# Attention and a gated MLP on one core: batch 2's local attention weights transposed by VectorE and DMA in place of TensorE, with new planner constants

## Chip, core and metric

One core of one Trainium2 chip. The metric is the device time of one execution in microseconds (us). The kernel before took 934.95 us, the median of 3 runs (934.14 to 935.41).

## What is computed

Two things in a row. First, for 8 batches and 8 heads (576 tokens, 64 numbers per head), a pooled attention (queries, keys and values averaged over 4 tokens) and a local attention (each token sees the tokens less than 4 places away) are added. Then the 4608 rows of 512 numbers go through a matrix to 2048 columns, a rational function of each element, and a matrix back to 512.

```python
out_d = sm_attn(q_d, k_d, v_d)                      # pooled by 4
out_up = np.repeat(out_d, factor, axis=2)
mask = np.abs(pos[:, None] - pos[None, :]) < factor
attn = softmax(np.where(mask, scores, -1e9))        # local
out = out_up + attn @ v

h = x @ w_in                                        # 4608x512 @ 512x2048
P = a[0] + a[1]*h + a[2]*h**2 + a[3]*h**3
Q = 1 + |b[0]|*|h| + |b[1]|*h**2
y = (P / (Q + 1e-6)) @ w_out
```

## The kernel before

**The MLP.** The tokens are cut into nine blocks of 512: the first 512 tokens of each of the 8 batches, and one block of all the remainders. A block has 16 steps (144 steps in all), one for each 128 of the 2048 columns. Step n has three parts. `h_part` (L1355 for block 0, with plain f32 operands; L1369 for the others, with each operand split into a high and a low part and three products) makes 128x512 values of h on TensorE (PE). `middle` takes them through six activations on ScalarE (ACT, all of them at L1383: three or four that read PSUM, a logarithm, an exponential) and seven operations on VectorE (DVE, L1399 to L1417); it leaves the high part `g` at L1408 and the low part at L1417. `o_part` (L1435, 12 matmuls) multiplies both into four PSUM banks. The step's `o_part` runs about two steps behind its `h_part`, so that the middle of a step has that long to finish. After a block's 16 steps ACT copies the four banks out (L1479) and SyncE (SP) stores them (L1482).

**The attention.** Batch b's attention is worked in two halves of two head pairs each (class `Half`; pairs a and o), and must end before block b's steps begin, since the block's rows come from it (`split_x`, L1308 on ACT and L1311 on DVE, makes the high and low parts). It is woven into the steps of earlier blocks: batch 2's lies in the steps of block 0's end and of block 1. A half is a chain: scores on PE (L572 or, with the mask added by PE, L562; L856 and L898 where DVE adds the mask), the row maximum on DVE, the exponentials on ACT (L648 from PSUM, L980 from SBUF, five a call, and L674 for the pooled part), the inverse sums (L684, L685) and the normalization on DVE (L730) and ACT (L709). Then the weights must be turned, keys onto the partitions, before PE can multiply them with the values (`weight_both`, one burst).

**Two ways to turn the local weights.** The constant `FLIP` says from which batch on the second way is used; it is 3 before.

- Batches 0 to 2, `turn`: for each pair PE transposes five 128x122 tiles into PSUM (L1033) and ACT copies them to SBUF as `et` (L1081). The weighting matmuls are those of L747.
- Batches 3 to 7, `flip`: the exponentials are written to a tile `eq` in another order of its columns; one DVE instruction transposes it in blocks of 32x32 into `fx` (L1109); SP sends `fx` to DRAM in four transfers (`fd`, L1121) and fetches it back in one (L1126) into `ef`, where each block stands at its place. The weighting matmuls are those of L741.

The pooled weights are transposed by PE in both (L1039 in `turn`, L1138 in `turn_pooled`). In batch 2 the mask is added by PE (`PEMASK`), before and after.

**What sets the order.** All operations are first recorded as tasks of a planner (`Plan`), each with an engine, a duration, the rooms that it reads and writes, and perhaps a due time. `Plan.run` places them on the engines one by one: of those that are ready on an engine, the one with the earliest latest-start time. What comes out is a fixed order of instructions for each engine; the due times are not looked at on the chip. The due time of step n's `h_part` is `due_h(n)`, which advances by `H_STEP` for each step after the 16th; `SPLIT_EARLY` and `ENDS` say how long before a block's first step its rows must stand ready, and `SCORES_EARLY` how long before that the two scores pieces are due. `FLIPSP` and `FLIPLAG` are what the planner takes for SP's issue of the four `fd` transfers and for the landing of `fd` and `ef`:

```python
            there = Room(None, [("D", c.b % 2, c.odd)])
            add("SP", FLIPSP, leave, (x,), (there,), lag=FLIPLAG[0])
            add("SP", 0.7, back, (there,), (y,), lag=FLIPLAG[1])
```

```python
            if b >= FLIP:
                for c in half_.cs:
                    half_.flip(c)
                half_.turn_pooled(bk)
                if q == 0:
                    todo_.append(begin_half(b, 1))
                elif b + 1 < B and AHEAD_S:
                    begun.append(begin_half(b + 1, 0))
            else:
                half_.turn(bk, bk, bk, lent[2])
```

Of the kernel before, what the change touches and what calls it, by code (L numbers as in the profile page):

```python
# [273 lines left out]
def attention_moe(  # L274
# [322 lines left out]
    def softmax_local(c, bk):  # L597
# [43 lines left out]
        def exps(j):  # L641
            for k in range(NW // 2):
                n = 2 * k + c.pos(j)
                dst, src = s.el.ap[:, k, c.pos(j), :], view[:, j, k, :]
                if c.b >= FLIP:
                    n = 5 * c.pos(j) + k
# [55 lines left out]
    def normalize(c):  # L702
# [22 lines left out]
        by = sm[:, :NW].unsqueeze(2).broadcast_to([P, NW, D])  # L725
        if c.b >= FLIP:
            e, by = s.eq.ap, sm[:, :NW].unsqueeze(1).unsqueeze(3).broadcast_to([P, 2, NW, QD])
# [6 lines left out]
    def window(c, x, w, o):  # L734
# [3 lines left out]
        for j in range(2):  # L738
            m = c.pos(j) * D
            if c.b >= FLIP:  # L740
                mms.append(nc.tensor.matmul(  # L741
# [74 lines left out]
    class Half:  # L816
# [22 lines left out]
        def scores(self, c, bk):  # L839

            flip = c.b >= FLIP

# [17 lines left out]

            add("PE", 0.95, issue, (c.slot.qk,), bk, due=self.due - SCORES_EARLY[c.odd] if c.b >= LATER else None)
            if c.b >= FLIP:
                n = NW // 2 * QD
# [20 lines left out]
        def scores_rest(self, bk):  # L884
# [32 lines left out]
            def issue():  # L917
# [17 lines left out]
                "PE", SREST, issue, (o.slot.qk, *(c.slot.pq for c in self.cs)), (*bk, bc),  # L935
                due=self.due - SCORES_EARLY[1]
            ).step = ROOM[0]
# [22 lines left out]
        def softmax(self, c):  # L960
            s = c.slot
            nm, sm = s.nm.ap, s.sm.ap
            if c.b >= FLIP:
                e, axis = s.eq.ap.rearrange("p b n k -> p n b k"), mybir.AxisListType.XY
# [139 lines left out]
        def flip(self, c):  # L1104
# [25 lines left out]
# [4 lines that stand above are left out]
# [154 lines left out]
    def due_h(n):  # L1288
        m = blocks[0].nstep
        return H0 + H_FIRST * min(n, m) + H_STEP * max(0, n - m)  # L1290

# [5 lines left out]
    def split_x(k, due=None):  # L1297
        blk = blocks[k]
        due = due or due_h(blk.first) - SPLIT_EARLY
        t = blk.t  # L1300
# [21 lines left out]
    def ahead(n):  # L1322
        return AHEAD * min(1.0, max(0, n - blocks[-1].first) / RAMP)
# [95 lines left out]
    def o_part(n, f, subs=range(4)):  # L1419
# [3 lines left out]
        fc = s * blk.fg + f  # L1423
        due = due_h(n) + O_LAG * H_STEP + 0.25 * f
        order = [[(m, sub) for m in (0, 2)] for sub in range(blk.nsub)] + [[(1, sub)] for sub in range(blk.nsub)]
        if n >= NS - KEEP:
            order = [[(m, sub) for m in (0, 2, 1)] for sub in subs]
            due = due_h(n) - ahead(n) + O_LAG * H_STEP + 20.0 * subs[0]
        for q, what in enumerate(order):
# [125 lines left out]
    def attend(b):  # L1555

        early, gap = (SPLIT_EARLY, QUAD_GAP) if b < LATER else ENDS
        last = due_h(blocks[b].first) - early - 3.0
# [38 lines left out]
    def begin_half(b, q):  # L1597
        early, gap = (SPLIT_EARLY, QUAD_GAP) if b < LATER else ENDS
        last = due_h(blocks[b].first) - early - 3.0
        bk = banks[0:2]  # L1600
        half_ = Half(b, q, last - (1 - q) * gap)
        half_.load()
        c = half_.cs[0]
        if b in PEMASK:
            scores(c, bk)
            softmax_local(c, bk)
        else:
            half_.scores(c, bk)
        return half_
# [75 lines left out]
O_LAG = 2.09  # L1685
H0 = 20.57
H_FIRST = 6.27
H_STEP = 6.13
SPLIT_EARLY = 8.0
QUAD_GAP = 42.0  # L1690
LATER = 2
ENDS = (8.0, 41.3)
SCORES_EARLY = (47.4, 41.0)
WARM = 0.6
EP_DVE = (1, 3)
LEAD = 13.84
# [16 lines left out]
SREST, ABOTH = 1.7, 2.2  # L1713
ROOM = (1.2, 1.2, 0.6)
LENT = (3, 2, 99)
FLIP = 3
AHEAD_S = 1
FLIPLAG = (2.5, 3.0)
FLIPSP = 2.4


_OUTS = [((NT, DM), "float32")]
# [69 lines left out]
```

## Time and profile before

| what | us |
|---|---|
| median of 3 runs (lowest, highest) | 934.95 (934.14, 935.41) |
| the profiled execution: its time | 936.64 |
| its span, first to last instruction | 934.8 |
| PE busy in the span | 920.8 |
| DVE busy | 852.0 |
| ACT busy | 784.2 |
| GpSimd (POOL) busy | 117.9 |

The span is what the profile's rows add up to; the profiled execution's own time lies 1.84 us above it, and 1.69 us above the median. "Busy" is the time in which an engine worked on at least one instruction. Matmuls follow each other faster than one takes (the next starts while the last drains), so what a row of PE costs is read from the start of one to the start of the next, and the same holds for short instructions on DVE and ACT.

### The profile page before, as it was taken

The page shows a single profiled execution, that of the slowest core. Times are in us where ns is not written, and L with a number is a line of the kernel's source. Part 1 is how long each engine was busy: PE and PEld are TensorE (multiplying, and loading weights), DVE is VectorE, ACT ScalarE, POOL GpSimd, SP SyncE. Part 2 cuts the span into 40 slices and gives each one's busy share as a digit, 9 for nine tenths or more (in the row PEclk, how much of TensorE's full clock was granted, in tenths as well). Part 3 has the DMA queues.
Part 4 walks back from the last instruction along what each step waited for, and adds up shares of the span by engine and source line. Part 5 has one row for each costly group of instructions (what it writes and reads, how often), then busy time and mean ns, then how long its engine had stood idle before and what let it go on. Part 6 is the DMA issues. An engine that isn't in the chain of part 4 may idle for free.

```text
span 934.8 us, 19294 instructions
## 1 busy us (share of the span) xinstructions
PE 920.8 (99%) x7149; PEld 728.7 (78%) x7149; DVE 852.0 (91%) x1381; ACT 784.2 (84%) x1906; POOL 117.9 (13%) x140
## 2 busy tenths in 40 slices
PE   8999999999999999999999999999999999999997
PEld 6666667788878888788878888888788888888886
DVE  8899999999879899889989998999898999988994
ACT  5899997989797979888897979797988887778772
POOL 3122021111120202020111112020201000000000
PEclk9999999999999999999999999999999999999999
DMA  9987453333464545363445436454522210001001
GB/s 319 325 265 186 138 129 73 102 73 90 101 131 119 101 126 125 95 123 96 112 112 143 77 98 136 114 105 120 129 73 45 57 46 1 1 0 46 1 1 45
DMA packets 58973, 97.62 MB, mean 104 GB/s; under 512 B 7744, under 2 KB 39552, under 8 KB 58880
## 3 DMA queue, kind: packets, MB, share of 16 engines
q1 hardware_dynamic: 41008, 76.30, 25.3%
q0 software_dynamic: 17728, 19.96, 15.5%
q8 instruction: 56, 0.92, 0.4%
q14 instruction: 37, 0.30, 0.1%
q10 hardware_dynamic: 144, 0.13, 0.0%
HBM read 80.38 MB, written 15.99 MB: 103 GB/s over the span
## 4 chain that ended last, share of the span: by engine, by line
PE 79%; ACT 13%; DVE 4%; issue 2%; DMA 1%; SPq 0%; DVEq 0%; ACTq 0%
PE psum L1435 36%; PE psum L1369 34%; ACT m L1383 5%; ACT eq L980 2%; ACT gb L1383 2%; PE psum L1355 2%; PE psum L741 1%; ACT epc L674 1%; ACT el L648 1%; PE psum L1189 1%; PE psum L1138 1%; PE psum L856 1%; DMA qk<-in_qk_dram 1%; DVE wb L472 1%; ACT xf L1479 1%
## 5 line engine op out<-in xcount | busy, mean ns | idle before, releaser
L1435 PE MATMUL psum<-wh,g 128*128 128x512 f32 x1072 | 364.9, 403 | 3.5 <-DVE g L1408 2.2
L1369 PE MATMUL psum<-xs,wh 128*128 128x512 f32 x1024 | 260.1, 392 | 0.0
L1383 ACT ACTIVATE m<-psum,cf 128x512 f32<-128x512 f32 x288 | 214.2, 751 | 37.9 <-PE psum L1369 28.2
L1435 PEld LDWEIGHTS psum<-wh,g 128*128 128x128 f32 x1072 | 200.3, 188 | 57.6 <-DVE g L1408 6.5
L1369 PEld LDWEIGHTS psum<-xs,wh 128*128 128x128 f32 x1024 | 191.0, 188 | 41.0 <-DVE xs L1311 0.3
L1435 PE MATMUL psum<-wl,g 128*128 128x512 f32 x536 | 209.7, 391 | 0.1
L1369 PE MATMUL psum<-xs,wl 128*128 128x512 f32 x512 | 138.4, 392 | 0.0
L1383 ACT ACTIVATE gb<-m,cf 128x512 f32<-128x512 f32 x134 | 100.8, 752 | 44.7 <-DVE m L1399 42.4
L1435 PEld LDWEIGHTS psum<-wl,g 128*128 128x128 f32 x536 | 100.8, 188 | 22.6 <-issue 2.3
L1383 ACT ACTIVATE gb<-psum,cf 128x512 f32<-128x512 f32 x134 | 107.9, 806 | 6.3 <-PE psum L1435 6.2
L1408 DVE TENSOR_TENSOR g<-m,m 128x512 fp32r<-128x512 f32 x134 | 92.1, 687 | 21.3 <-ACT m L1383 15.3
L1369 PEld LDWEIGHTS psum<-xs,wl 128*128 128x128 f32 x512 | 95.2, 188 | 20.4 <-issue 0.4
L1399 DVE SCALAR_TENSOR_TENSOR m<-m,cf,m 128x512 f32<-128x512 f32 x144 | 107.4, 746 | 2.9 <-ACT m L1383 2.7
L528 POOL DMA_DIRECT2D pq<-in_qkp_dram x84 | 75.2, 942 | 221.8 <-DMA pq<-in_qkp_dram 135.2
L1416 DVE TENSOR_TENSOR m<-m,m 128x512 f32<-128x512 f32 x144 | 99.2, 689 | 1.8
L1404 DVE TENSOR_TENSOR m<-m,m 128x512 f32<-128x512 f32 x144 | 98.5, 684 | 0.9 <-ACT m L1383 0.7
L1405 DVE TENSOR_TENSOR m<-m,gb 128x512 f32<-128x512 f32 x134 | 92.1, 687 | 3.6 <-ACT gb L1383 0.6
L1417 DVE TENSOR_TENSOR g<-m,m 128x512 fp32r<-128x512 f32 x134 | 91.8, 685 | 3.3 <-PE psum L747 0.5
L1383 ACT ACTIVATE m<-gb 128x512 f32<-128x512 f32 x134 | 87.9, 656 | 7.7 <-DVE m L1404 6.5
L1411 DVE SCALAR_TENSOR_TENSOR m<-m,g 128x512 f32<-128x512 f32 x134 | 92.0, 686 | 2.1
L1383 ACT ACTIVATE m<-psum 128x512 f32<-128x512 f32 x144 | 88.5, 615 | 0.0
L528 POOL DMA_DIRECT2D vpc<-in_vp_dram x42 | 35.5, 846 | 363.7 <-DMA vpc<-in_vp_dram 266.2
(118 smaller groups left out, 1052.0 us busy)
## 6 DMA issues: line engine op xcount, KB each, us to landing
qk<-in_qk_dram SPq DMA_DIRECT2D x32, 590.0 KB, 4.7
pq<-in_qkp_dram POOLq DMA_DIRECT2D x84, 144.0 KB, 3.4
vw<-in_vw_dram SPq DMA_DIRECT2D x32, 320.0 KB, 3.8
out_dram<-xf SPq DMA_DIRECT2D x35, 256.0 KB, 4.0
vpc<-in_vp_dram POOLq DMA_DIRECT2D x42, 168.0 KB, 3.5
fd<-fx SPq DMA_DIRECT2D x80, 80.0 KB, 1.8
ef<-fd SPq DMA_DIRECT2D x20, 320.0 KB, 2.9
sx<-in_w_in_dram SPq DMA_DIRECT2D x5, 1024.0 KB, 11.3
```

Source lines behind the costliest of these rows:

```text
L528: lambda d=dst, x=x: nc.gpsimd.dma_start(out=d.ap, in_=x, accum_op=ALU.add),
L980: nc.scalar.activation(out=e[:, n], in_=e[:, n], func=AF.Exp, bias=nm[:, n : n + 1], scale=scale, accum_out=sm[:, n : n + 1],)
L1369: nc.tensor.matmul(ph.ap[:, f * t : (f + 1) * t], lhsT=(high, low)[j][0][fc].ap[:, c, :], rhs=blk.x[i].ap[:, c, :] if blk.b is not None el ...
L1383: return add("ACT", cost, lambda: nc.scalar.activation(out=to, in_=in_, func=func, **kw), (room_in, cf, *more), (out_,))
L1399: lambda: v.scalar_tensor_tensor(out=tb.ap, in0=tq.ap, scalar=b1, in1=tb.ap, op0=ALU.mult, op1=ALU.add),
L1404: add("DVE", 0.61, lambda: v.tensor_tensor(out=ta.ap, in0=ta.ap, in1=tq.ap, op=ALU.mult), (ta, tq), (ta,))
L1405: add("DVE", 0.61, lambda: v.tensor_tensor(out=ta.ap, in0=ta.ap, in1=u, op=ALU.add), (ta, gh), (ta,))
L1408: add("DVE", 0.61, lambda: v.tensor_tensor(out=gh.ap, in0=ta.ap, in1=tq.ap, op=ALU.mult), (ta, tq), (gh,))
L1411: lambda: v.scalar_tensor_tensor(out=tb.ap, in0=tb.ap, scalar=CONE, in1=gh.ap.bitcast(F32), op0=ALU.add, op1=ALU.mult),
L1416: add("DVE", 0.61, lambda: v.tensor_tensor(out=tb.ap, in0=ta.ap, in1=tb.ap, op=ALU.subtract), (ta, tb), (tb,))
L1417: add("DVE", 0.61, lambda: v.tensor_tensor(out=gl.ap, in0=tb.ap, in1=tq.ap, op=ALU.mult), (tb, tq), (gl,))
L1435: nc.tensor.matmul(ob[sub].ap, lhsT=g[i].ap[:, f0 : f0 + P], rhs=flat((high, low)[j][1][fc].ap), start=(fc == 0 and m == 0), stop=(fc == N ...
```

## The change

`FLIP` goes from 3 to 2: batch 2's four pairs take the second way too. That also moves the start of the next half's scores in front of the weighting burst of batch 2 (the branch shown above), and it starts batch 3's first half within batch 2's second. The other lines are constants of the planner.

```diff
-H_STEP = 6.13
-SPLIT_EARLY = 8.0
+H_STEP = 6.2
+SPLIT_EARLY = 10.0
 QUAD_GAP = 42.0
 LATER = 2
-ENDS = (8.0, 41.3)
-SCORES_EARLY = (47.4, 41.0)
+ENDS = (10.1, 43.3)
+SCORES_EARLY = (48.1, 38.0)
...
-FLIP = 3
+FLIP = 2
 AHEAD_S = 1
-FLIPLAG = (2.5, 3.0)
-FLIPSP = 2.4
+FLIPLAG = (1.9, 2.8)
+FLIPSP = 1.8
```

Since every due time moves, the order changes in many places from step 2 on; the first 40 us stay as they are on PE. Three places matter here.

**PE, batch 2's first half, from the last transposes to the weighting burst.** `el` and `et` are the local weights before and after PE's transposes, `epc` the pooled ones, `ef` the weights as fetched back by DMA; L1369 and L1435 are the MLP's matmuls. Before:

```order
L1369 MATMUL psum<-xs_0_108,wh_8_92 128x512 x4
L1033 MATMUL psum<-ident,el_146 128x122
L1033 MATMUL psum<-ident,el_152 128x122
L1039 MATMUL psum<-ident,epc_141 112x112
L1369 MATMUL psum<-xs_1_109,wh_8_92 128x512 x4
L1435 MATMUL psum<-wh_4_98,g_125 128x512 x4
L1369 MATMUL psum<-xs_0_108,wl_8_64 128x512 x4
L747 MATMUL psum<-et_147,vw_145 64x58 x2
L747 MATMUL psum<-et_153,vw_151 64x58 x2
```

and with the change:

```order
L1369 MATMUL psum<-xs_0_108,wh_8_92 128x512 x4
L1435 MATMUL psum<-wh_4_98,g_125 128x512 x4
L1369 MATMUL psum<-xs_1_109,wh_8_92 128x512 x4
L1369 MATMUL psum<-xs_0_108,wl_8_64 128x512 x4
L741 MATMUL psum<-ef_0_183,vw_145 64x64 x2
L741 MATMUL psum<-ef_1_184,vw_151 64x64 x2
```

The transposes of the local weights are gone from PE (the eight that stood some rows further up too), and the pooled ones have moved up: from the last pooled transpose to the burst there stand now 24 matmuls of L1435, 28 of L1369 and the scores of the next half (44 of the 52 matmuls behind those scores), where there were 4 and 8 and no scores.

**DVE, the same half, around its normalization.** L730 normalizes a pair's weights, L1109 is the new transpose, the other rows are the MLP's middle (`g` at L1408 and L1417 is what PE waits for). Before:

```order
L684 TENSOR_SCALAR smb_138<-smb_138 128x2x13
L685 RECIPROCAL smb_138<-smb_138 128x2x13
L1408 TENSOR_TENSOR g_122<-m_116,m_120 128x512
L730 TENSOR_TENSOR el_146<-el_146,smb_138 128x640
L730 TENSOR_TENSOR el_152<-el_152,smb_138 128x640
L1411 SCALAR_TENSOR_TENSOR m_118<-m_118,g_122 128x512
L1416 TENSOR_TENSOR m_118<-m_116,m_118 128x512
L1399 SCALAR_TENSOR_TENSOR m_119<-m_121,cf,m_119 128x512
L1417 TENSOR_TENSOR g_124<-m_118,m_120 128x512
```

and with the change:

```order
L730 TENSOR_TENSOR eq_154<-eq_154,smb_138 128x640
L1408 TENSOR_TENSOR g_123<-m_117,m_121 128x512
L1109 STREAM_TRANSPOSE fx_181<-eq_148 128x2x2x160
L1411 SCALAR_TENSOR_TENSOR m_119<-m_119,g_123 128x512
L1399 SCALAR_TENSOR_TENSOR m_118<-m_120,cf,m_118 128x512
L1416 TENSOR_TENSOR m_119<-m_117,m_119 128x512
L1404 TENSOR_TENSOR m_116<-m_116,m_120 128x512
L1417 TENSOR_TENSOR g_125<-m_119,m_121 128x512
L1405 TENSOR_TENSOR m_116<-m_116,gb_126 128x512
L1408 TENSOR_TENSOR g_122<-m_116,m_120 128x512
L1411 SCALAR_TENSOR_TENSOR m_118<-m_118,g_122 128x512
L1109 STREAM_TRANSPOSE fx_181<-eq_154 128x2x2x160
```

The normalization comes one step of the MLP earlier than it did, and each of the two transposes stands between a step's L1408 and its L1417.

**ACT, batch 5's first half (the same in batches 4, 6 and 7).** L980 are the exponentials of the second pair's local weights, L674 those of the pooled weights, and `m<-gb` is a step's last activation, after which DVE can make `g`. Before:

```order
L980 ACTIVATE eq_154,smb_138<-eq_154,nmb_136 128x2x32 x5
L1383 ACTIVATE m_116<-psum,cf 128x512
L1383 ACTIVATE gb_126<-psum,cf 128x512
L1383 ACTIVATE gb_128<-m_118,cf 128x512
L1383 ACTIVATE m_119<-psum,cf 128x512
L674 ACTIVATE epc_141,smb_138<-psum,nmb_136 128x3x48 x6
L1383 ACTIVATE m_120<-gb_128 128x512
```

and with the change:

```order
L980 ACTIVATE eq_154,smb_138<-eq_154,nmb_136 128x2x32 x5
L1383 ACTIVATE gb_126<-psum,cf 128x512
L1383 ACTIVATE gb_128<-m_118,cf 128x512
L1383 ACTIVATE m_119<-psum,cf 128x512
L1383 ACTIVATE m_120<-gb_128 128x512
L674 ACTIVATE epc_141,smb_138<-psum,nmb_136 128x3x48 x6
L1383 ACTIVATE m_121<-psum 128x512
```

The pooled exponentials now follow the step's last activation in the first half of a batch. In the second half it is the other way round: there they followed it before, and stand in front of it now; the step ahead of that place holds none of the attention's exponentials and no copy, where the step ahead of the old place holds the four copies of the output (L1479).

On SP's queue the 20 new transfers of batch 2 stand between the loads of its second half and of batch 3. The second pair's fetch (`ef`) stands behind the load of a scores operand (L511), which itself waits until PE has done the next half's scores.

## Rows read from the trace of the kernel before

**Rows 1.** Busy by stretch: length, PE, weight loads, DVE, ACT, POOL, clock, DMA share, GB/s.
```profile
40.00:110.00 70.00, 69.67 (x513) 42.65 (x512) 68.63 (x105) 68.54 (x166) 14.51 (x16) 1.00 0.72 203
110.00:160.00 50.00, 48.95 (x302) 33.00 (x301) 49.33 (x76) 44.70 (x101) 7.74 (x9) 1.00 0.48 125
160.00:260.00 100.00, 99.97 (x909) 80.61 (x911) 93.27 (x150) 86.35 (x238) 15.50 (x18) 1.00 0.40 91
260.00:360.00 100.00, 98.98 (x794) 80.51 (x788) 91.40 (x153) 87.46 (x233) 15.51 (x18) 1.00 0.49 114
360.00:460.00 100.00, 99.89 (x847) 81.84 (x850) 92.23 (x155) 86.27 (x229) 15.56 (x18) 1.00 0.49 113
460.00:560.00 100.00, 99.39 (x827) 81.34 (x821) 93.02 (x156) 87.31 (x234) 15.47 (x18) 1.00 0.49 113
560.00:660.00 100.00, 100.00 (x846) 81.75 (x842) 92.02 (x154) 86.15 (x228) 15.53 (x18) 1.00 0.48 113
660.00:760.00 100.00, 99.23 (x755) 81.17 (x747) 91.82 (x153) 85.93 (x220) 7.76 (x9) 1.00 0.29 70
...
760.00:840.00 80.00, 80.00 (x355) 66.28 (x354) 72.99 (x111) 62.02 (x98) 0.00 (x0) 1.00 0.04 14
```

**Rows 2.** PE's timeline at batch 2's transposes: start, length, line, operands, count.
```profile
187.57 1.00 PE L1033 MATMUL psum<-ident,el 122*128 122x122 f32 x8
188.44 1.21 PE L1369 MATMUL psum<-xs,wh 128*128 128x512 f32 x4
...
196.12 0.37 PE L1033 MATMUL psum<-ident,el 122*128 122x122 f32 x2
196.34 0.26 PE L1039 MATMUL psum<-ident,epc 112*112 112x112 f32 x1
```

**Rows 3.** PE's timeline, a weighting burst of batch 2 and one of batch 3.
```profile
199.27 0.92 PE L747 MATMUL psum<-et,vw 64*64 64x58 f32 x48
...
201.34 0.50 PE L1435 MATMUL psum<-wh,g 128*128 128x512 f32 x1
...
297.74 0.93 PE L741 MATMUL psum<-ef,vw 64*64 64x64 f32 x48
...
299.82 0.50 PE L1435 MATMUL psum<-wh,g 128*128 128x512 f32 x1
```

**Rows 4.** DVE: the group of the transposes (busy, mean ns), and one in the timeline.
```profile
L1109 DVE STREAM_TRANSPOSE fx<-eq 128x640 f32<-128x640 f32 x20 | 16.8, 839 | 0.0
...
281.01 0.84 DVE L1109 STREAM_TRANSPOSE fx<-eq 128x640 f32<-128x640 f32 x1
281.77 0.65 DVE L1417 TENSOR_TENSOR g<-m,m 128x512 fp32r<-128x512 f32 x1
```

**Rows 5.** ACT, 165 to 255 us: the larger copies of batch 2's transposed weights.
```profile
L1081 ACT COPY et<-psum 128x488 f32<-128x488 f32 x4 | 2.2, 632 | 0.0
```

**Rows 6.** SP's timeline for one pair of batch 3, and the landing time of all 20 fetches.
```profile
281.88 1.81 SPq L1121 DMA_DIRECT2D fd<-fx  x4
285.29 0.34 SPq L1126 DMA_DIRECT2D ef<-fd  x1
...
DMA to landing us min/median/max: 2.6/2.9/3.3
```

**Rows 7.** Batch 5's first half in the timelines of ACT, DVE and PE; idle time in brackets.
```profile
464.48 2.02 ACT L1479 COPY xf<-psum 128x512 f32<-128x512 f32 x4
466.37 0.75 ACT L1383 ACTIVATE gb<-m,cf 128x512 f32<-128x512 f32 x1
...
474.57 0.37 ACT L674 ACTIVATE epc<-psum,nmb 128x144 f32<-128x144 f32 x1
...
476.70 0.65 ACT L1383 ACTIVATE m<-gb 128x512 f32<-128x512 f32 x1
...
476.86 0.18 DVE L684 TENSOR_SCALAR smb<-smb 128x26 f32<-128x26 f32 x1 [2.52 <-ACT epc L674]
...
478.13 0.51 PE L1435 MATMUL psum<-wh,g 128*128 128x512 f32 x1 [0.61 <-DVE g L1408]
```

## The prediction

> **What bounds the kernel now.** I read the busy times by stretch first. PE has nearly no idle time in any of them from 40 us on: it lacks 0.33 us of 70, then 1.05 of 50, then 0.03 of 100, and in the five stretches of batches 3 to 7 (260 to 760 us) 1.02, 0.11, 0.61, 0.00 and 0.77, together 2.51 us [rows 1]. The reader should see that DVE and ACT are far from idle too, and where: DVE is busy 98% from 40 to 160 us (68.63 of 70, 49.33 of 50), 93% from 160 to 260, where batch 2's attention lies, and 92% after that; ACT stands at 86 to 87% from 160 on. "Busy" overlaps on PE, so the rate tells more: where only the MLP is left, 355 matmuls start in 80 us, 0.225 us each [rows 1]. PE is thus the bound, with DVE close behind it in the first 160 us, and the granted clock is 1.00 throughout, so no term comes from the clock.
>
> The page "Perfetto Trace Analysis" of the Trainium skill (section "Identifying the Most-Contended Engine") warns that the matmul busy share is no good measure of how near PE is to its limit, and takes occupancy for DVE. By that rule DVE could be the engine to spare, and this change loads it; it stands behind the slower rival below, and the rate just read is what speaks against it here.
>
> Then I read PE's timeline where the change cuts, DVE's and SP's where it adds, and last the places where PE does wait in batches 3 to 7, which the new due dates move.
>
> **The change part by part.**
>
> *PE loses 20 transposes.* In batch 2's first half the group of eight costs 188.44 - 187.57 = 0.87 us from its start to the next instruction's, the group of two 196.34 - 196.12 = 0.22 [rows 2]. The second half has the same two groups: 2 x 1.09 = 2.2 us. PE has no idle time in that stretch (0.03 us), so all of it is on the path: **-2.2 us**. The bursts that weight the values cost the same in both ways, 201.34 - 199.27 = 2.07 and 299.82 - 297.74 = 2.08 us [rows 3]: nothing.
>
> *ACT loses the copies* of those tiles, 2.2 us for the four larger ones [rows 5] and at most as much again for the four small ones. No PE wait of that stretch is there to shorten, so I take 0; the bound below is also 0, since PE cannot gain more than its 0.03 us of idle time.
>
> *DVE gains four transposes* of 0.84 us each, which cost 281.77 - 281.01 = 0.76 from start to start [rows 4]: 3.0 us. They go into the stretch with 93.27 us of DVE work, and that stretch gets 2.2 us shorter on PE: 96.3 of 97.8 us, 98.5% busy. Each stands between the L1408 and the L1417 of a step, so the MLP's `g` waits behind it, and PE's L1435 behind that. What such a load does to PE is seen in the two stretches before: at 98.0% DVE, PE lacks 0.33 us in 70 (0.5 in 100); at 98.7%, 1.05 in 50 (2.1 in 100) [rows 1]. The new wait lies between 0 and 2.1 us; nearest are these two rows, and 98.5% lies between them. I take **+1.0 us**. The 1.05 us that PE already lacks between 110 and 160 us may go or double, since batch 1 and the start of batch 2 move by a step against the weights' preparation: 0, with 1 us to either side.
>
> *The transfers.* From the first `fd` issue to the fetch pass 285.29 - 281.88 = 3.4 us, and the fetch lands after 2.9, at most 3.3: 6.7 us from the end of a DVE transpose [rows 6]. In the new order 52 of the MLP's matmuls and the scores stand on PE between the last pooled transpose and the burst, 52 x 0.225 = 11.7 us, and the second DVE transpose comes at about that place. On SP the second pair's fetch stands behind a load that waits for the scores of the next half, but 44 matmuls (9.9 us) follow those scores before the burst, and the fetch needs 0.3 + 3.3 of them. The cover is 9.9 against 3.6, so I take 0. Were it gone, PE would wait some 3.6 us twice, 7.2 us. What else queues on SP there, the loads for the next half, is late by the same issue times, 4 x (1.81 + 0.34) = 8.6 us spread over 100 us; batches 3 to 7 carry the same load on that queue with no PE wait for it. The planner's new figures (1.8, 1.9, 2.8) lie at what these rows measure.
>
> *The due dates.* They touch batches 3 to 7, where PE lacks 2.51 us. One such place: ACT works off six pooled exponentials (474.57 to 476.70, 2.1 us) ahead of the step's last activation; DVE stands 2.52 us at L684, which needs them, with L1408 queued behind it, and PE waits 0.61 us for that `g` [rows 7]. In the new order ACT does the step's last activation first and the pooled exponentials after it, in the first half of a batch: that wait goes. In the second half the pooled exponentials now come first, so the wait could reappear there. But the step ahead of the old place held the four output copies, 466.37 - 464.48 = 1.9 us of ACT [rows 7], and the step ahead of the new place holds nothing of the attention. ACT is 1.9 us further on, and PE's waits are 0 to 1.02 us. So most of them should go. The first half keeps the copies in its step and may keep some wait: I take two thirds of 2.51, **-1.7 us**. Bounds: all of it goes (-2.5), or a wait like the largest, 1.02, comes in each of the five batches (+2.6).
>
> **Sum.** -2.2 + 1.0 - 1.7 = -2.9 us. Against the profiled execution's 936.64 us that is 933.7; it lies 1.69 us above the median of the runs, so on the runs' scale 932.05, say **932.1 us**.
>
> **The rivals.**
>
> 1. *All the waits go* (DVE's transposes fit into its gaps, the batches' waits vanish): -2.2 - 2.5 = -4.7, 930.2 us, and 929.2 if the 1.05 us of 110 to 160 go as well. For it: DVE has 6.7 us free from 160 to 260 [rows 1]. Against: part of that free time is waiting for ACT, as at L684, and can't be filled at will. Chance 0.20.
>
> 2. *PE's gain becomes PE's wait.* The new wait takes its upper bound (+2.1) and the batches' waits only change place (0): -0.1, 934.9 us, no change. For it: the stretch from 110 to 160 shows just such a rate of waiting at the same DVE load. Against: the ACT order is lighter at the new place. Chance 0.13.
>
> 3. *The trade at its face value.* A pair's five transposes cost PE 1.09 / 2 = 0.54 us and DVE 0.76; if DVE's microseconds are worth as much as PE's, four pairs lose 4 x 0.22 = 0.9 us: 935.8, no change that shows. [...] Against: from 160 us on PE has no idle time and DVE has. Chance 0.05.
>
> 4. *Slower: DVE takes over as the bound.* If the chain of DVE operations from step to step is what sets the pace from 110 to 260 us (the batch's normalization comes a step earlier, on top of the last weights' preparation), PE's 2.2 us are free time and the four transposes go onto the path whole: +3.0, 938.0 us. It decides from the point at which DVE's gaps there are under 0.8 us each and stand at the wrong places. For it: 98.7% before 160 us. Against: 93% after. Chance 0.08. Late fetches (cover of 9.9 us gone, +7.2 - 2.9, 939.3 us) I give 0.02.
>
> **How the numbers follow.** A measurement of this kernel tells about 0.2%, 1.87 us, from no change: faster is below 933.1, slower above 936.8. The forecast has 0.52, of which 0.04 falls on the wrong side of 933.1. Faster: 0.48 + 0.20 = 0.68. Same: 0.04 + 0.13 + 0.05 = 0.22. Slower: 0.08 + 0.02 = 0.10. The range takes in rival 1 to nearly its end (929.0) and rivals 2 and 3 to 935.7, which leaves the slower cases and a little at the low end outside.
>
> **What the changed profile would show.** L1033 x40 instead of x60 and L1109 x24 instead of x20. From 160 to 260 us PE's small matmuls come 2.2 us shorter; DVE is over 96% busy; PE's waits for L1408 or L1417 there sum to about 1 us, and every us more comes off the gain. The burst of L741 in batch 2 has no idle time before it. In batches 3 to 7 PE's idle time falls from 2.51 to under 1 us, and DVE's wait at L684 moves to the second halves. I am wrong if PE waits more than 2 us between 110 and 260 us, if the waits of the batches come back in the second halves at 0.5 us or more each, or if a burst waits for `ef`.

## The result, and the profile after

The changed kernel takes 943.69 us, the median of four runs (942.02 to 944.11), the kernel before 934.93 beside it: the ratio is 1.0089, 95% interval 1.0073 to 1.0105. The forecast was 932.1, range 929.0 to 935.7: it is wrong in sign. The profiled execution has a span of 942.3 us against 934.8.

First the same stretches as in [rows 1], after the change:

```profile
110.00:160.00 50.00, 48.62 (x340) 33.14 (x339) 49.59 (x78) 44.89 (x110) 8.05 (x9) 1.00 0.52 139
160.00:260.00 100.00, 96.73 (x809) 76.80 (x808) 92.74 (x149) 81.05 (x222) 15.46 (x18) 1.00 0.46 109
260.00:360.00 100.00, 98.48 (x811) 79.88 (x810) 90.57 (x152) 86.19 (x221) 15.57 (x18) 1.00 0.50 115
360.00:460.00 100.00, 99.20 (x817) 80.74 (x817) 90.76 (x152) 85.76 (x227) 15.51 (x18) 1.00 0.49 113
460.00:560.00 100.00, 99.18 (x817) 80.75 (x816) 92.02 (x154) 85.92 (x229) 15.47 (x18) 1.00 0.47 113
560.00:660.00 100.00, 99.44 (x819) 80.92 (x818) 92.18 (x154) 86.18 (x229) 15.46 (x18) 1.00 0.47 111
660.00:760.00 100.00, 98.11 (x771) 80.67 (x770) 91.16 (x153) 85.71 (x227) 7.83 (x10) 0.98 0.30 71
```

PE lacks 3.27 us between 160 and 260, where it lacked 0.03, and 5.59 in the five stretches after that, where it lacked 2.51. From 160 us on DVE and ACT are busy for as long as before or less (at most 0.16 us more in a stretch): it is not more work that holds PE up, something waits. The groups of waits name it (engine, line, what it waited for; us in all, times, the longest). After:

```profile
PE psum L741 <- ACT gb L1383: 4.2, 2, 2.3
PE psum L741 <- ACT m L1383: 1.5, 3, 0.6
ACT xs L1308 <- DMA ef<-fd: 12.4, 4, 5.3
ACT xs L1308 <- issue: 5.5, 2, 3.0
```

and of these four, all that the kernel before has:

```profile
ACT xs L1308 <- DMA ef<-fd: 7.9, 4, 3.1
ACT xs L1308 <- issue: 1.4, 1, 1.4
```

The weighting burst L741 waits 5.7 us for ACT's reads of PSUM (L1383), and ACT itself has stood idle 17.9 us at L1308 for the fetch `ef` or with no cause shown ("issue"), against 9.3 before. L1308 is the split's copy: for block b it rounds the rows `xf` into `xs`. The largest case is batch 2's second half; the timelines of SP, ACT, PE and DVE (start, length, line, operands; idle time in brackets). SP:

```profile
233.68 2.74 SPq L1121 DMA_DIRECT2D fd<-fx  x4
236.46 0.45 SPq L511 DMA_DIRECT2D qk<-in_qk_dram  x1
238.10 0.34 SPq L1126 DMA_DIRECT2D ef<-fd  x1
```

ACT:

```profile
235.32 0.78 ACT L1383 ACTIVATE gb<-psum,cf 128x512 f32<-128x512 f32 x1
241.40 0.62 ACT L1308 CAST xs<-xf 128x512 fp32r<-128x512 f32 x1 [5.29 <-DMA ef<-fd]
...
243.98 0.58 ACT L1383 ACTIVATE m<-psum 128x512 f32<-128x512 f32 x1
244.45 0.77 ACT L1383 ACTIVATE m<-psum,cf 128x512 f32<-128x512 f32 x1
245.12 0.78 ACT L1383 ACTIVATE gb<-psum,cf 128x512 f32<-128x512 f32 x1
```

PE:

```profile
242.58 1.07 PE L1369 MATMUL psum<-xs,wl 128*128 128x512 f32 x4
245.95 0.93 PE L741 MATMUL psum<-ef,vw 64*64 64x64 f32 x48 [2.30 <-ACT gb L1383]
```

DVE:

```profile
242.05 0.69 DVE L1311 TENSOR_TENSOR xs<-xf,xs 128x512 fp32r<-128x512 f32 x1 [3.90 <-ACT xs L1308]
```

Read those of PE, ACT and SP upward. The burst borrows one of the two banks of the MLP's h (`bc = Loan()` in `weight_both`), so it waits until ACT has read that step's h; the last read starts at 245.12. The reads are late because ACT sat idle for 5.3 us from 236.1 on, with the copy at the head of its queue. The copy starts at 241.40, 3.3 us after the issue of the fetch `ef`, as the fetch lands. The burst does not wait for `ef` itself, which was there 4.5 us earlier. DVE stands behind the same copy: the subtraction L1311 that follows it waits 3.90 us, with the step's L1404, L1405 and L1408 queued behind it.

Why does a copy of the rows wait for `ef`? `fx`, the two `ef` and the first half of `xs` lie in the same place of SBUF: by the program's offsets `fx` has bytes 0 to 2559 of a partition, the `ef` 2560 to 7679, and this first of the block's four copies writes 0 to 2047. By its bytes it must wait for the transfers that read `fx`, not for the fetch. ACT's order with the counters that an instruction waits for shows more:

```
320 L1383 ACTIVATE gb1_127<-psum,cf_134 128x512 [waits PE_49]
321 L1308 CAST xs0_0_104<-xf0_1_107 128x512 [waits DMAHW4_49,DMAHW5_49,DMAHW3_49,DMAHW6_49,DMAHW2_49,DMAHW7_49,DMAHW1_49,DMAHW0_49]
```

The value it waits for on DMAHW1 is the one that the fetch of `ef_1` brings that counter to. The planner knows nothing of that: in its plan the copy follows the leaving transfers by `FLIPLAG[0]`, 3.7 us after their first issue by the new constants and 4.9 by the old ones, while on the chip the fetch lands 7.7 us after it here, and 6.7 in batch 7 (735.12 to the copy's 741.81). The old constants were 1.2 us longer, and that hid part of the rule the plan lacks.

How the planned starts and the chip's go apart shows where the time is lost. The planner gives each task a start when the program is built; this is the chip's start of L1408 less the planned one, in us, at every 16th step (the last two columns: the planner's end of the program, and the trace's span):

```
step               16     32     48     64     80     96    112    128 | planned   span
before           1.30   1.13   0.97   1.27   0.97   1.52   1.68   1.28 |  930.0   934.8
changed          1.04   6.12   7.38   9.06  10.24  11.16  14.24  14.53 |  924.4   942.3
lags_alone       1.26   1.03   3.14   5.68   7.49  10.32   9.90   9.83 |  929.8   943.2
copy_moved       1.55   3.56   4.38   5.34   5.94   6.47   6.82   6.55 |  924.4   934.3
lags_copy_moved  1.39   1.19   1.75   1.86   1.97   2.07   2.25   1.62 |  929.8   935.0
fetch_after_both 1.62   3.63   7.45   8.26   9.16   9.38  10.62  10.92 |  924.4   938.7
planned_return   1.60   2.29   2.37   2.79   3.29   3.73   5.27   4.92 |  922.0   930.2
```

The kernel before keeps to its plan. The changed one has a plan that is 5.6 us shorter and falls behind it in every batch, 13.1 us more by the end (17.9 against 4.8): -5.6 + 13.1 = +7.5, the difference of the spans.

Of the 5.1 us lost in batch 2, 1.1 come before the copy, on DVE's timeline:

```profile
232.81 0.84 DVE L1109 STREAM_TRANSPOSE fx<-eq 128x640 f32<-128x640 f32 x1 [1.19 <-DMA fd<-fx]
```

The second pair's transpose must wait for the first pair's `fx` to leave. The fetch that follows that landing was issued 5.4 us after the first transfer (227.29 to 232.73); in [rows 6] it was 3.4.

### The profile page after: what moved, and what is told of

It is laid out like the page before. It is cut to its first block, busy times and chain, and to the rows that moved or that the text cites. A ratio compares the mean times of both kernels' runs of the same rounds, so it can differ in the third digit from the quotient of the medians.

```text
span 942.3 us, 19295 instructions
## 1 busy us (share of the span) xinstructions
PE 923.5 (98%) x7129; PEld 728.6 (77%) x7129; DVE 855.0 (91%) x1385; ACT 782.0 (83%) x1898; POOL 118.1 (13%) x140
## 4 chain that ended last, share of the span: by engine, by line
PE 58%; DVE 19%; ACT 11%; DMA 5%; issue 4%; SPq 1%; DVEq 0%; ACTq 0%; POOLq 0%
PE psum L1435 27%; PE psum L1369 24%; ACT m L1383 4%; PE psum L1355 3%; DMA fd<-fx 3%; DVE g L1408 2%; ACT eq L980 2%; ACT gb L1383 2%; DVE m L1416 2%; DVE m L1411 2%; ACT epc L674 2%; DVE m L1399 2%; DVE m L1405 2%; SPq L1121 1%; DVE xs L1311 1%
## 5 line engine op out<-in xcount | busy, mean ns | idle before, releaser
L1435 PE MATMUL psum<-wh,g 128*128 128x512 f32 x1072 | 366.4, 403 | 1.5 <-DVE g L1408 0.5
L1369 PE MATMUL psum<-xs,wh 128*128 128x512 f32 x1024 | 260.7, 392 | 1.9 <-ACT gb L1383 0.5
L1383 ACT ACTIVATE m<-psum,cf 128x512 f32<-128x512 f32 x288 | 215.7, 756 | 48.4 <-PE psum L1369 32.3
L1435 PEld LDWEIGHTS psum<-wh,g 128*128 128x128 f32 x1072 | 200.3, 188 | 55.8 <-issue 4.6
L1369 PEld LDWEIGHTS psum<-xs,wh 128*128 128x128 f32 x1024 | 190.5, 188 | 45.5 <-DVE xf L791 2.3
L1435 PE MATMUL psum<-wl,g 128*128 128x512 f32 x536 | 209.5, 391 | 0.0
L1369 PE MATMUL psum<-xs,wl 128*128 128x512 f32 x512 | 137.2, 390 | 0.0
L1383 ACT ACTIVATE gb<-m,cf 128x512 f32<-128x512 f32 x134 | 100.7, 751 | 24.9 <-DVE m L1399 22.2
L1383 ACT ACTIVATE gb<-psum,cf 128x512 f32<-128x512 f32 x134 | 108.5, 812 | 13.0 <-PE psum L1435 12.7
L1435 PEld LDWEIGHTS psum<-wl,g 128*128 128x128 f32 x536 | 100.9, 188 | 21.6 <-issue 1.9
L1408 DVE TENSOR_TENSOR g<-m,m 128x512 fp32r<-128x512 f32 x134 | 91.9, 686 | 27.5 <-ACT m L1383 23.0
L1369 PEld LDWEIGHTS psum<-xs,wl 128*128 128x128 f32 x512 | 96.0, 188 | 20.2
L1404 DVE TENSOR_TENSOR m<-m,m 128x512 f32<-128x512 f32 x144 | 98.1, 681 | 1.9 <-ACT m L1383 1.9
L1383 ACT ACTIVATE m<-gb 128x512 f32<-128x512 f32 x134 | 87.9, 656 | 12.4 <-DVE m L1404 11.7
L1405 DVE TENSOR_TENSOR m<-m,gb 128x512 f32<-128x512 f32 x134 | 91.9, 686 | 3.1 <-ACT gb L1383 0.2
L1417 DVE TENSOR_TENSOR g<-m,m 128x512 fp32r<-128x512 f32 x134 | 91.6, 684 | 3.2
L1383 ACT ACTIVATE m<-psum 128x512 f32<-128x512 f32 x144 | 89.3, 620 | 0.0
```

Source lines behind the costliest of these rows:

```text
L1369: nc.tensor.matmul(ph.ap[:, f * t : (f + 1) * t], lhsT=(high, low)[j][0][fc].ap[:, c, :], rhs=blk.x[i].ap[:, c, :] if blk.b is not None el ...
L1383: return add("ACT", cost, lambda: nc.scalar.activation(out=to, in_=in_, func=func, **kw), (room_in, cf, *more), (out_,))
L1404: add("DVE", 0.61, lambda: v.tensor_tensor(out=ta.ap, in0=ta.ap, in1=tq.ap, op=ALU.mult), (ta, tq), (ta,))
L1405: add("DVE", 0.61, lambda: v.tensor_tensor(out=ta.ap, in0=ta.ap, in1=u, op=ALU.add), (ta, gh), (ta,))
L1408: add("DVE", 0.61, lambda: v.tensor_tensor(out=gh.ap, in0=ta.ap, in1=tq.ap, op=ALU.mult), (ta, tq), (gh,))
L1417: add("DVE", 0.61, lambda: v.tensor_tensor(out=gl.ap, in0=tb.ap, in1=tq.ap, op=ALU.mult), (tb, tq), (gl,))
```

## Experiments

Each result is the median time of a kernel, then its ratio to the kernel before, run beside it, with a 95% interval.

The theories: **A**, the copy L1308, planned too early, holds ACT; **B**, the new due dates place the burst badly; **C**, batch 2's own transposes and transfers cost the time; **D**, the lent bank is planned too tightly.

### The three parts alone, and the copy planned later

`flip2_alone`: the kernel before with one line changed.

```diff
-FLIP = 3
+FLIP = 2
```

> Batch 2's weights go by DVE and transfers; due dates and planned transfer times stay as before. Theory A (the planned transfer times let ACT's first copy of the split, L1308, stand too early; it holds ACT until the fetch of ef lands, the lent bank is read late, the burst L741 waits): nothing of that here, PE gains 2.2 us and gives up 0 to 2 to DVE, 932.7 to 935.5 us, waits of L741 under 0.5 us in sum. Theory B (the due dates alone place the burst too early): the same 932.7 to 935.5. Theory C (batch 2 by DVE and transfers costs it by itself): 3.5 us or more lost between 160 and 260 us, 937 us or more.

947.68 us, 1.0121 (1.0106 to 1.0136). `dates_alone`: the four lines of due dates.

```diff
-H_STEP = 6.13
-SPLIT_EARLY = 8.0
+H_STEP = 6.2
+SPLIT_EARLY = 10.0
...
-ENDS = (8.0, 41.3)
-SCORES_EARLY = (47.4, 41.0)
+ENDS = (10.1, 43.3)
+SCORES_EARLY = (48.1, 38.0)
```

> Only the due dates are new. Theory A: ACT waits at L1308 as before, about 1.6 us a batch, L741 under 0.5 us in each batch; 933.5 to 936.5 us. Theory B: L741 waits 0.5 to 2 us in the second half of most of batches 3 to 7, 938 to 941 us. Theory C: about 935 us.

950.37 us, 1.0150 (1.0135 to 1.0165). `lags_alone`: the two lines of transfer times.

```diff
-FLIPLAG = (2.5, 3.0)
-FLIPSP = 2.4
+FLIPLAG = (1.9, 2.8)
+FLIPSP = 1.8
```

> Only the planned times of the transfers are new (1.8 + 1.9 for leaving, 2.8 for the return, in place of 2.4 + 2.5 and 3.0). Theory A: ACT's wait at L1308 grows by 1.2 us a batch, from 7.9 in all to 13 or more, and L741 begins to wait in the second halves; 936 to 940 us. Theories B and C: 934 to 936 us, no wait of L741.

945.08 us, 1.0095 (1.0080 to 1.0110). `changed_copy_later`: the changed kernel with one addition to the planner's rule (`gap`).

```diff
         if p.lag is not None:
-            return p.lag
+            return p.lag + (3.0 if p.engine == "SP" and t.engine == "ACT" and p.lag == FLIPLAG[0] else 0.0)
```

> The changed kernel, but the planner takes 3.0 us more from the leaving transfers to an ACT operation that writes over their source, so that L1308's first copy comes 3 to 6 activations later; all else as changed. Theory A: ACT's wait at L1308 falls from 17.9 us to under 5, L741's waits from 6.5 us to under 1.5, 936 to 938.5 us. Theories B and C: L741 still waits 4 us or more, 942 us or more. Rival D (the lent bank is simply planned too tightly against ACT's reads, whatever ACT does before): L741 still waits 3 us or more, 940 to 943 us.

943.15 us, 1.0071 (1.0054 to 1.0088).

Each part alone loses as much as all three together or more. A's ranges failed in all three; of the other theories' ranges only C's 937 or more held, for `flip2_alone`. A alone foresaw that `lags_alone` loses, but put it at 936 to 940. The groups of waits say that they lose in different ways; one row of `flip2_alone`:

```profile
PE psum L1435 <- DVE g L1408: 6.1, 10, 1.3
```

and two of `dates_alone`:

```profile
PE psum L1435 <- DVE g L1408: 9.1, 10, 1.7
PE psum L1435 <- DVE nmb L698: 2.8, 4, 0.7
```

These two have no wait of L741, and the planner itself ends them late, at 937.0 and 941.2 against 930.0 for the kernel before: new due dates, new transfer times and `FLIP` were set together, and one without the others makes another, worse plan (7.0 of the 11.5 us that `flip2_alone` loses are in its plan's end, so C's hit says little). So such an undoing part by part doesn't share out the loss. `changed_copy_later` suffers from the same: L741's waits fall to 0.2 us and ACT's at L1308 (for the fetch or with no cause shown) to 1.4, as A said. But its time lies in the range of B and C and not in A's: the added 3 us give a plan that ends at 934.2, and new waits come elsewhere:

```profile
PE psum L1369 <- ACT gb L1383: 4.9, 4, 1.5
```

(at 475.6 us, for one, twenty exponentials of L980 stand on ACT in a row, 468.2 to 474.8, ahead of the read that PE waits for). Only `lags_alone` is a clean case: its planned end is that of the kernel before within 0.2 us, and it falls 8.6 us further behind it. It also shows that the copy's place counts, not the length of its wait. ACT in batch 4's second half, before the change:

```profile
436.24 0.68 ACT L1383 ACTIVATE m<-psum,cf 128x512 f32<-128x512 f32 x1
436.81 0.60 ACT L1383 ACTIVATE m<-psum 128x512 f32<-128x512 f32 x1
437.28 0.79 ACT L1383 ACTIVATE gb<-psum,cf 128x512 f32<-128x512 f32 x1
440.87 0.62 ACT L1308 CAST xs<-xf 128x512 fp32r<-128x512 f32 x1 [2.80 <-DMA ef<-fd]
```

and in `lags_alone`:

```profile
436.31 0.77 ACT L1383 ACTIVATE m<-psum,cf 128x512 f32<-128x512 f32 x1
440.07 0.62 ACT L1308 CAST xs<-xf 128x512 fp32r<-128x512 f32 x1 [2.99 <-DMA ef<-fd]
440.59 0.68 ACT L1383 ACTIVATE m<-psum,cf 128x512 f32<-128x512 f32 x1
441.17 0.59 ACT L1383 ACTIVATE m<-psum 128x512 f32<-128x512 f32 x1
441.65 0.78 ACT L1383 ACTIVATE gb<-psum,cf 128x512 f32<-128x512 f32 x1
```

The wait is 2.8 us in the one and 3.0 in the other (in all 9.3 and 11.1; I had expected 13). Before, three reads of the bank stand ahead of the copy; with the new transfer times they stand behind it. DVE's subtraction waits for the copy there too, 10.7 us in all against 0.3, and PE waits 5.5 us for ACT's reads and 4.0 for DVE (L791), where before it had no such wait. The page "PSUM — Partial Sum Buffer" of the Trainium skill (section "Engine vs sequencer instructions") says that ScalarE's queue is strictly first in, first out; the trace agrees, since that step's first read was done at 436.31, so its bank was ready, and the other three still come only behind the copy.

### The copy moved, nothing replanned

To leave the plan as it is, the finished order is edited: `moved_` holds the first copy of each block from batch `FLIP` on and DVE's subtraction behind it. PE's, SP's and POOL's orders stay as they were.

```diff
...
-    todo = plan.run()
+    todo = sorted(plan.run(), key=lambda t: (t.start + 4.0 * (t in moved_), t.n))
```

`copy_moved` is the changed kernel with this, `dates_lags_copy_moved` the same with `FLIP = 3`, `lags_copy_moved` is `lags_alone` with it.

> The changed kernel with PE's, SP's and POOL's orders untouched: only ACT's first copy of each split (L1308) and DVE's subtraction behind it (L1311) stand about 4 us of work further back, in batches 2 to 7. Theory A (the copy holds ACT until the fetch of ef has landed, so ACT's reads of the lent bank are late): L741's waits fall from 5.7 us to under 1, ACT's at L1308 from 17.9 to under 4; between the planner's start and the chip's start of L1408 the difference grows by about 2 us over the run and no more by 13; 929 to 934 us, so faster than both kernels. Theory C (DVE's transposes and the late fetch of batch 2 cost it): the 5 us of batch 2 stay, 936 to 940 us. Theory B and rival D (due dates, or a lent bank planned too tightly): L741's waits stay, 941 us or more.

> As copy_moved, but batch 2's weights by PE as before the change (FLIP = 3). It tells the price of DVE's four transposes by itself: theory A with PE's 2.2 us as forecast and DVE's new wait of 0 to 2 us: 0 to 2.2 us slower than copy_moved, 931 to 935 us. Theory C: 1 to 5 us faster than copy_moved.

> lags_alone with only ACT's first copy and DVE's subtraction 4 us further back. Theory A: the 9 us that lags_alone lost go, the same as the kernel before within 2 us; L741 and L1369 wait under 1 us in sum. Any theory by which the planned transfer times place the burst or the transposes badly, and not the copy: 941 us or more.

936.09 us, 1.0002 (0.9992 to 1.0011); 936.45, 1.0005 (0.9996 to 1.0014); 936.53, 1.0007 (0.9998 to 1.0016). The loss is gone in both pairs: from 1.0089 to 1.0002 and from 1.0095 to 1.0007. B and D fall, since PE's order with its due dates and its lent bank is untouched. C falls by the table and not by the time: 936.09 lies in its range (936 to 940), but of the 5.1 us lost in batch 2, which C would keep, 2.0 stay, though the batch still goes by DVE. The copy and the subtraction behind it were moved together, so these runs don't divide the loss between ACT's queue and DVE's. Batch 2's second half in `copy_moved`, on ACT:

```profile
239.68 0.58 ACT L1383 ACTIVATE m<-psum 128x512 f32<-128x512 f32 x1
240.15 0.77 ACT L1383 ACTIVATE m<-psum,cf 128x512 f32<-128x512 f32 x1
240.81 0.78 ACT L1383 ACTIVATE gb<-psum,cf 128x512 f32<-128x512 f32 x1
242.27 0.62 ACT L1308 CAST xs<-xf 128x512 fp32r<-128x512 f32 x1 [0.67 <-issue]
```

and on PE:

```profile
243.86 0.93 PE L741 MATMUL psum<-ef,vw 64*64 64x64 f32 x48
```

The reads come 4.3 us earlier than in the changed kernel, the copy even 0.9 us later, and the burst has no wait. But by A `copy_moved` was expected at 929 to 934 and `dates_lags_copy_moved` at 931 to 935, and neither is faster than the kernel before; `copy_moved` still falls 5 us behind its plan, by 2.0 us in batch 2 and about 0.6 a batch after that.

### The kernel before with the copy further forward

```diff
...
-    todo = plan.run()
+    todo = sorted(plan.run(), key=lambda t: (t.start + -2.0 * (t in moved_), t.n))
```

> The kernel before (FLIP = 3, old due dates, old transfer times), PE's, SP's and POOL's orders untouched; only ACT's first copy of each split and DVE's subtraction behind it stand 2 us of work further forward, ahead of two or three of ACT's reads of the MLP's bank, as the copy stands in the changed kernel. Theory A: ACT's wait at L1308 grows from 9.3 us to 17 or more, those reads come late, and PE begins to wait behind them in the second halves of batches 3 to 7 (L741, L1369 or L1435 for ACT, 3 us or more in sum); 940 to 946 us. Theories B, C and D (the new due dates, batch 2's transposes, a lent bank planned too tightly): nothing of theirs is in this kernel, so as fast as the kernel before within 1.5 us.

938.33 us, 1.0025 (1.0016 to 1.0035): slower, as A has it against the others, but by 2.3 us and not by 4 or more, and not in the way expected. The copy waits less, for another transfer:

```profile
437.36 0.62 ACT L1308 CAST xs<-xf 128x512 fp32r<-128x512 f32 x1 [1.34 <-DMA fd<-fx]
```

Two us further forward it stands ahead of the fetch in the program, and then it waits for the leaving transfers and no longer for that fetch; in SP's order that fetch now waits for ACT (a counter that it hasn't in the kernel before). So which of the two waits for the other is set by their order in the program alone.

### The fetch behind the copy

`pairs_` names for each such fetch ACT's copy; the fetch is written into the program just behind it. Each engine keeps its order in `fetch_after_copy`.

```diff
...
-    todo = plan.run()
+    todo = sorted(plan.run(), key=lambda t: (max(t.start, pairs_[t].start + 1e-6) if t in pairs_ else t.start, t.n))
```

> The changed kernel with the order of every engine and queue untouched; in the program the fetch of the second pair's ef now stands behind ACT's first copy of the split in place of ahead of it, so that the copy waits for the leaving transfers alone and the fetch for the copy. Theory A, in the form that the wait for the landing of ef (whose bytes the copy does not touch) is what holds ACT: ACT's wait at L1308 falls from 17.9 us to under 6, L741's waits from 5.7 to under 1.5, 931 to 936 us. If ACT's reads are late for another reason (rival D, the lent bank planned too tightly) or if the fetch, now behind ACT, comes too late for the burst: 940 us or more.

> As fetch_after_copy, with due dates set anew by the planner's own end (H_STEP 6.07, SPLIT_EARLY 10.74, ENDS 5.64 and 40.92, SCORES_EARLY 48.2 and 42.43, QUAD_GAP 38.63, LATE 1.13), which lies 2.4 us before the changed kernel's and as early as planned_return's. Theory A: 929 to 933 us, as planned_return. If the wait for ef is not what matters: 936 or more.

938.18 us, 1.0022 (1.0012 to 1.0032), and 941.20, 1.0057 (1.0045 to 1.0070): both slower than A's numbers. In the first, three quarters of the loss are gone (from 1.0089 to 1.0022), though no engine's order was touched: that the wait for `ef` holds ACT is shown. What remains sits mostly in batch 2 (4.5 of the 6.5 us that it falls behind its plan), in the waits:

```profile
PE psum L741 <- ACT gb L1383: 2.1, 1, 2.1
DVE xs L1311 <- issue: 4.0, 1, 4.0
```

DVE's subtraction of the same chunk stands behind the fetch in the program, and now it waits: it stands idle from 237.3 to 241.27, 3.4 us after the fetch's issue at 237.84, with the step's operations queued behind it. The retuned version was expected at 929 to 933; there L1311 waits 9.0 us in five places, for `ef` or with no cause shown. With the fetch behind the subtraction too (`pairs_` names the subtraction):

> As fetch_after_copy, but the fetch stands behind DVE's subtraction (L1311) as well; ACT, DVE, PE and POOL keep their orders, on SP a load of qk comes ahead of that fetch. Theory A (what stands behind the fetch in the program waits for its landing, ACT's copy or DVE's subtraction alike): DVE's wait of 4.0 us at L1311 and L741's of 2.1 go, 934 to 936.5 us, as copy_moved. If the fetch is now too late for the burst, or batch 2's transposes are what is left: L741 waits 2 us or more, 938 us or more.

> retuned_fetch_after_copy with the fetch behind DVE's subtraction too. Theory A: the 9.0 us of DVE's waits at L1311 fall under 2, and the 941.2 us of retuned_fetch_after_copy fall to 931 to 935. If the loss there has another cause: 939 us or more.

939.24 us, 1.0040 (1.0028 to 1.0053), a miss for A (the other reading gave 938 or more, with the fetch too late for the burst), and 935.95, 1.0006 (0.9997 to 1.0015), just above A's range. Batch 2 comes out as A says: no wait of L1311 for the fetch, no wait of the burst, 3.6 us behind the plan at step 32 as in `copy_moved`. The retuned version gains the 5 us that it had lost; in place of L1311's waits for the fetch stand 4.3 us for the copy, and the burst waits 3.2 for `ef`. But from batch 3 on the fetch is now late itself. SP's timeline in batch 3 of `fetch_after_both`:

```profile
331.65 1.77 SPq L1121 DMA_DIRECT2D fd<-fx  x4
336.28 0.35 SPq L511 DMA_DIRECT2D qk<-in_qk_dram  x1
339.73 0.34 SPq L1126 DMA_DIRECT2D ef<-fd  x1
```

and PE's:

```profile
342.75 0.86 PE L741 MATMUL psum<-ef,vw 64*64 64x64 f32 x42 [1.94 <-DMA ef<-fd]
```

8.1 us from the first transfer to the fetch in place of 3.4 [rows 6], and the burst waits for `ef` for the first time (4.4 us in all). So either order has its price, unless the plan counts it.

### The rule in the plan

`planned_return`: the copy follows the fetch in the plan as it does on the chip, and the due dates are set anew by the planner's own end; `planned_return_flip3` the same for `FLIP = 3`.

```diff
...
-            add("SP", 0.7, back, (there,), (y,), lag=FLIPLAG[1])
+            returned[c.b % 2] = add("SP", 0.7, back, (there,), (y,), lag=FLIPLAG[1])
...
-            add("ACT", 0.11 + t / 1390, lambda hi=hi, x=x: nc.scalar.copy(out=hi.ap, in_=x), (lo,), (hi,), due=due)
+            first = add("ACT", 0.11 + t / 1390, lambda hi=hi, x=x: nc.scalar.copy(out=hi.ap, in_=x), (lo,), (hi,), due=due)
+            if c == 0 and blk.b is not None and blk.b >= FLIP:
+                first.preds[returned[blk.b % 2]] = True
+                returned[blk.b % 2].succs.append(first)
...
```

> The changed kernel (FLIP = 2, new transfer times), but the planner itself knows that ACT's first copy of a split follows the fetch's landing, and the due dates are set anew under that rule (H_STEP 6.09, SPLIT_EARLY 9.57, ENDS 6.13 and 40.55, SCORES_EARLY 48.2 and 42.43, QUAD_GAP 38.34, LATE 1.17). Its planned end lies 2.5 us before the changed kernel's planned end and 8 us before that of the kernel before. Theory A (the copy is what the plan had wrong; with it right the chip keeps to the plan): the chip falls behind the plan by 1 to 4 us over the run as in lags_copy_moved and the kernel before, 926 to 931 us, faster than both kernels. If other things that the plan does not know cost as much as in copy_moved (5 us): 931 to 934. If the planned end tells nothing: 936 or more.

> As planned_return, but batch 2's weights by PE (FLIP = 3), with due dates set anew for that (H_STEP 6.3, SPLIT_EARLY 11.33, ENDS 6.78 and 42.27, SCORES_EARLY 43.91 and 46.46, QUAD_GAP 40.77, LATE 0.83); planned end 0.8 us after planned_return's. Theory A: 927 to 932 us. If batch 2's transposes on DVE cost more on the chip than they save: as fast as planned_return or faster.

931.70 us, 0.9957 (0.9943 to 0.9971), and 932.69, 0.9969 (0.9958 to 0.9981): both beat both kernels. Both lie 0.7 us above what A gave (926 to 931, and 927 to 932), the first in the range for a plan that lacks other things too: the copy was the largest thing the plan had wrong and not the only one. The rule and new due dates came together here, and no run has the new due dates without either the rule or a fetch moved in the program; the two `retuned` kernels, whose plans end at 922.0 as well, took 941.20 and 935.95. The chip falls 3.3 us behind `planned_return`'s plan from step 16 to 128 (13.5 in the changed kernel), and PE's idle time in batches 3 to 7 is 0.86 us. Four of its stretches:

```profile
160.00:260.00 100.00, 98.49 (x878) 79.31 (x877) 96.02 (x155) 85.31 (x237) 15.51 (x18) 1.00 0.49 113
260.00:360.00 100.00, 99.71 (x819) 81.22 (x818) 92.21 (x155) 88.10 (x238) 15.53 (x18) 1.00 0.48 113
360.00:460.00 100.00, 99.97 (x823) 81.92 (x822) 92.66 (x156) 87.70 (x231) 15.56 (x18) 1.00 0.50 115
660.00:760.00 100.00, 99.52 (x727) 81.75 (x727) 92.79 (x154) 86.41 (x214) 7.76 (x9) 1.00 0.29 72
```

## Why the prediction was wrong

**PE is the bound, not DVE: right as far as the runs show.** DVE did not take over as the slower rival had it. Between 160 and 260 us it is busy 92.74 us in the changed kernel, and in `copy_moved`:

```profile
160.00:260.00 100.00, 99.32 (x844) 78.87 (x846) 95.60 (x153) 84.24 (x229) 15.51 (x18) 1.00 0.50 113
```

The four transposes are some 3.0 us more work for DVE, and `copy_moved`, which has them, is no slower than `dates_lags_copy_moved`, which has not (936.09 and 936.45). The page "Perfetto Trace Analysis" of the Trainium skill, in the section that the prediction names, would have named DVE by its occupancy (95.60 us in this row, against 78.87 of weight loads on PE); the two runs speak against that here.

**PE's 20 transposes, -2.2 us: right in size.** From each L1033 to the next instruction's start it is 6.47 us for 60 in `dates_lags_copy_moved` and 4.53 for 40 in `copy_moved`: 1.94. That all of it was on the path is not shown, as the next numbers say.

**DVE's transposes, +1.0 us: fits, within wide bounds.** With the step before it made -1.2. Between `copy_moved` and `dates_lags_copy_moved` it is -0.4 us, which their intervals can't tell from none; between `planned_return` and `planned_return_flip3`, whose due dates differ too, -1.0. The sum had no term for the transposes' wait for `fx`: 1.4 us in all in the changed kernel, none before. The burst costs the same in both ways, also right: 243.86 to 245.92 (the L1435 behind it), 2.06 us.

**The transfers, 0: the step that failed.** "The cover is 9.9 against 3.6, so I take 0", and "The planner's new figures (1.8, 1.9, 2.8) lie at what these rows measure". The first held, since no burst waited for `ef`. The second held for the rows it was read from; in batch 2 of the changed kernel the 3.4 us became 4.4 and 5.4. Both are beside the point. I asked only whether the burst would wait for `ef`, in batch 2's first half. I didn't ask what else waits for these transfers and what is queued behind it: the copy on ACT, with the reads of the lent bank behind it, and DVE's subtraction. Standing 4 us further back, these two alone take the loss from 1.0089 to 1.0002. The trace of before showed the wait, 9.3 us of ACT's idle time at L1308 (7.9 for `ef`, 1.4 with no cause shown), as idle time of an engine that is not the bound. And I took shorter transfer times as more exact, while the copy follows a landing that comes 6.7 to 7.7 us after the first issue: the new 3.7 are further from that than the old 4.9.

**The due dates, -1.7 us: failed too, behind the same wait.** In `copy_moved` PE's idle time between 260 and 760 us is 1.25 us against 2.51, so the idle time that I saw did go, most of it. The time didn't follow: its span is 0.5 us below that of the kernel before, and by the medians it is as fast (1.0002), where the idle times and the transposes would give more than 2. Part of it lies where the view counts no idle time: between starts the 128 L1355 take 50.77 us in place of 48.92. For batches 3 to 7 I found no one place.

**The signs named as wrong** came: PE waits over 2 us between 110 and 260 (it lacks 4.65), and PE waits in the second halves of batches 4 to 7 (0.56, 0.62, 0.35 and 1.89 us), though for the burst's bank and not for `g`. The third, a burst that waits for `ef`, did not come. Of the rivals, "late fetches" (0.02) was nearest: right about the transfer, wrong about who waits for it, and its 939.3 is too low.

## What to carry to other kernels

When a change shortens a planned wait, list everything that waits for that event, on every engine, and read in the trace when each starts; what matters is which work stands behind it in the queue. A planner's constant that is too long may stand in for a rule that it lacks: make it exact only together with the rule. And where due dates were set for one plan, a part undone alone is another plan; move one task in the finished order to find a cause.

## What was not expected of the hardware

The wait before batch 7's burst cost more than its length. The busy view of the changed kernel by 5 us (PE first, the clock third from the end), around the bursts of batches 2 and 7:

```profile
245.00:250.00 5.00, 4.05 (x113) 3.62 (x114) 4.93 (x9) 4.28 (x9) 0.00 (x0) 1.00 0.15 37
...
745.00:750.00 5.00, 3.98 (x106) 3.77 (x107) 4.56 (x8) 3.71 (x7) 0.00 (x0) 0.69 0.02 7
```

and PE's timeline of the second:

```profile
746.02 0.97 PE L741 MATMUL psum<-ef,vw 64*64 64x64 f32 x46 [1.89 <-ACT gb L1383]
...
749.32 0.79 PE L1435 MATMUL psum<-wh,g 128*128 128x512 f32 x1
```

After 1.89 us of idle PE the granted clock is 0.69 on average of the 5 us from 745 on: from 746.87 to 750.27 it is 0.50 (1.2 GHz), and the burst takes 3.30 us in place of 2.06. After 2.30 us of idle time in batch 2 it stays at 1.00. Two other runs differ in the same way: in `fetch_after_both` the clock is 0.50 from 343.67 to 347.07, behind the 1.94 us of idle PE shown above; in `fetch_after_copy` it stays at 1.00 behind the 2.07 us before batch 2's burst. So an idle time of about 2 us may or may not cost clock. Of the four runs of the changed kernel three have a mean clock of 0.998 and take 943.58 to 944.11 us; the one at 1.000 takes 942.02; by that one run the clock's share is 1.6 to 2.1 of the 8.8 us, as an estimate.
